# Third batch's values and late queries loaded ahead of the key and query turns, and its values cast ahead of its queries

## The chip, the cores and the metric

The kernel runs on one core of a Trainium2 chip. The metric is the time on the device in microseconds (us), the median over several executions. A separate profiled execution gives the trace from which everything about engines and transfers is read.

## The reference

Grouped-query attention followed by a gated MLP with a spatial mixing step. There are 8 batches, 16 query heads, 4 key/value heads, a sequence of 384 and a head dimension of 64. The width of the model and of the hidden layer is 1024.

```python
k = np.repeat(k, group, axis=1); v = np.repeat(v, group, axis=1)
scores = scale * np.matmul(q, k.transpose(0, 1, 3, 2))
scores = scores - np.max(scores, axis=-1, keepdims=True)
attn = np.exp(scores)
attn = attn / (np.sum(attn, axis=-1, keepdims=True) + 1e-09)
x = np.matmul(attn, v)            # then heads beside each other: [B, S, 1024]

h = np.maximum(x @ w_in, 0.0)
u, v = h[..., :512], h[..., 512:]
v_n = (v - mean(v)) / np.sqrt(var(v) + 1e-06)
v_s = np.einsum('ts,bsd->btd', w_spatial, v_n) + b_spatial[None, :, None]
out = (u * v_s) @ w_out
```

## The kernel before

One program does both parts, batch after batch, and lays the MLP of one batch beside the attention of the next. The order of instructions on every engine is written out by the program when it is built; nothing is reordered afterwards.

**Attention.** A batch is cut into 18 units: three query tiles (`qt`), two groups of heads (`j`), three key tiles (`kt`). Units are numbered through all batches, so batch 0 has 0 to 17, batch 1 has 18 to 35 and batch 2, the third, begins at 36. From unit 21 on, three units are done at a time, which I call a step and name by its first unit (24, 27, ..., 36, 39, 42). `units` issues the score matmuls (`sc`, L281) from the turned keys `kT` and the turned queries `qT`. `exp` on ScalarE gives `aT`. `weigh` (L301) multiplies with the values `v1` into `av`, and VectorE divides into `x` (L315, L317).

**MLP.** `v_part` (`pv`, L357) and `u_part` (`pu`, L438) multiply the turned `x`, named `xt`, by `w_in`. `s_part` (`psp`, L457) does the spatial mixing, and POOL multiplies into `gT` (L474). `o_part` (`po`, L496) multiplies by `w_out`. `gated` strings these together, and `pour` deals them out between the attention's instructions by a budget of TensorE time.

**How a batch's inputs get ready.** Loads bring float32 into staging tiles. They are `load_k`, `load_v` and `load_q`, and a query load can be cut by tiles: `(0,)` is the first query tile and `(1, 2)` are the late ones. POOL casts to float16 (`cast_k`, `cast_q`, `cast_v` at L187 to L208). Then the keys and queries are turned. For batches 0 and 1 TensorE turns them. From the third batch on, SP issues transposing DMAs: `k_send` (L250) and `q_send` (L258). The turned x goes the same way from batch 1 on (`x_send`, L341). The values need no turn; `cast_v` writes straight into `v1`, of which there are two, used by even and odd batches.

**What sets the order around the change.** `at(n, f, ...)` puts a call into a list under a unit number. In a step the lists of its three units are called one after the other, at one fixed place in the step, each list in the order in which it was written:

```python
for u in range(n, n + NT):
    for f, args in todo.pop(u, []):
        f(*args)
```

SP takes its DMAs one after the other, and POOL its casts and its own DMAs. So a call's place in these lists is its place in the queue of its engine. The output projection's weights `w_out` are loaded by two DMAs that POOL issues in step 24 (L169).

The third batch needs, in order: `kT` and the first tile of `qT` for `j` = 0 at step 36, the first tile of `qT` for `j` = 1 at step 39, its values in `v1` for the first `weigh` at the end of step 36, and the late tiles of `qT` for `j` = 0 at step 42.

Of the kernel before, what the change touches and what calls it, by code (L numbers as in the profile page):

```python
# [18 lines left out]
def kernel(  # L19
# [52 lines left out]
    pool, dve, act, sp = nc.gpsimd, nc.vector, nc.scalar, nc.sync  # L72
# [521 lines left out]
    def at(n, f, *args):  # L594
        todo.setdefault(n, []).append((f, args))
# [82 lines left out]

    at(20, cast_k, 2, pool)
    at(22, cast_q, 2, 0, pool, (0,))  # L680
    at(24, k_send, 2)
    at(24, q_send, 2, 0, 0, 1)
    at(26, cast_q, 2, 1, pool, (0,))
    at(26, q_send, 2, 1, 0, 1)
    at(26, load_w_out, 0, DH)
    at(26, load_w_out, DH, DM)
    at(29, load_q, 2, 0, sp, (1, 2))
    at(29, load_v, 2)
    at(31, load_q, 2, 1, sp, (1, 2))
    at(36, cast_v, 2, pool)  # L690
    for j, n in ((0, 34), (1, 36)):
        at(n, cast_q, 2, j, pool, (1, 2))
        at(n + 1, q_send, 2, j, 1, NT)
# [346 lines left out]
```

## Time and profile before

| | before |
|---|---|
| median of 3 runs | 238.40 us |
| lowest and highest | 238.39, 239.18 us |
| profiled execution, its own time | 238.65 us |
| span of the trace | 237.1 us |
| TensorE busy | 230.4 us (97%) |
| ScalarE, VectorE, POOL busy | 170.0, 143.8, 102.2 us |
| SP's DMA queue (q1), share of the 16 DMA engines' time | 68.9% |
| POOL's DMA queue (q0), the same | 12.3% |

The profiled execution takes 1.55 us longer than its span, which is what lies around the program. In the trace, PE is TensorE's matmuls and PEld its weight loads; DVE is VectorE, ACT ScalarE, POOL GpSimd and SP SyncE; SPq marks the issue of a DMA by SP, which then runs on the 16 DMA engines. L and a number is a line of the kernel.

### The profile page before, as it was taken

Reading aid. Unit: us, or ns where it says so; the run is one execution under the profiler, and the core shown is the slowest. Engines: PE = TensorE matmul, PEld = TensorE weight load, DVE = VectorE, ACT = ScalarE, POOL = GpSimd, SP = SyncE. Lnnn points to the kernel's source line nnn. Section 1 sums busy time; section 2 is a strip of 40 time slices with the busy share of each in tenths; the row PEclk is TensorE's granted clock in tenths of the full one; section 3 lists DMA queues with packets and bytes.
Section 4 is the critical chain, followed back from the end, with each engine's and each line's share of the span. In section 5 each row is a group of like instructions: output and inputs, shape, how many; then the busy total and the mean of one; then the engine's idle time right before and its main releaser. Section 6 shows DMA issues by size and latency. Waiting matters only on the chain.

```text
span 237.1 us, 5954 instructions
## 1 busy us (share of the span) xinstructions
PE 230.4 (97%) x2317; PEld 124.3 (52%) x2317; DVE 143.8 (61%) x382; ACT 170.0 (72%) x350; POOL 102.2 (43%) x149
## 2 busy tenths in 40 slices
PE   7899999999999999999999999999999999999993
PEld 6555655545554545555464555554465455545542
DVE  2668774676447674566646576376744667367561
ACT  2899989959897869977797776986697776401212
POOL 3489493642556442275045800575032500460740
PEclk9999999999999999999999999999999999999999
DMA  6999959999999999699988899479912543240266
GB/s 186 289 300 308 275 152 160 169 317 260 296 211 237 258 351 171 214 199 309 188 257 214 241 214 294 68 271 158 255 27 44 114 164 79 48 177 0 86 229 222
DMA packets 67757, 47.48 MB, mean 200 GB/s; under 512 B 48368, under 2 KB 60576, under 8 KB 67728
## 3 DMA queue, kind: packets, MB, share of 16 engines
q1 hardware_dynamic: 62800, 39.86, 68.9%
q0 software_dynamic: 3952, 6.42, 12.3%
q10 hardware_dynamic: 976, 0.82, 1.1%
q8 instruction: 18, 0.29, 0.5%
q14 instruction: 11, 0.09, 0.1%
HBM read 25.95 MB, written 12.58 MB: 163 GB/s over the span
## 4 chain that ended last, share of the span: by engine, by line
PE 91%; DMA 4%; DVE 2%; issue 0%; ACTq 0%; ACT 0%
PE pu L438 18%; PE pv L357 17%; PE po L496 17%; PE sc L281 15%; PE av L301 14%; PE psp L457 7%; DMA q<-in_q_dram 2%; DMA qT<-q 2%; PE qps L240 1%; PE xps L334 1%; DVE x L317 1%; DVE qT L218 0%; DVE osb L218 0%; DVE q L208 0%; ACTq L124 0%
## 5 line engine op out<-in xcount | busy, mean ns | idle before, releaser
L293 ACT ACTIVATE aT<-sc 128x512 f16<-128x512 f32 x288 | 147.5, 617 | 31.4 <-PE sc L281 30.8
L301 PEld LDWEIGHTS <-aT 128*128 128x128 f16 x1152 | 47.0, 97 | 17.3 <-issue 2.3
L357 PE MATMUL pv<-w_in,xt 128*128 128x512 f16 x192 | 51.0, 380 | 0.1
L301 PE MATMUL av<-v,aT 128*128 128x65 f16 x1152 | 50.5, 193 | 0.1
L496 PE MATMUL po<-w_out,gT 128*128 128x512 f16 (+2 forms) x200 | 50.5, 371 | 0.0
L438 PE MATMUL pu<-xt,w_in 128*128 128x384 f16 x256 | 49.9, 327 | 0.0
L401 POOL TENSOR_SCALAR vn<-vr,rstd,nmr 128x512 f16<-128x512 f32 x23 | 17.6, 779 | 67.0 <-DVE nmr L396 45.6
L474 POOL TENSOR_TENSOR gT<-vs,uT 128x384 f16<-128x384 f32 x31 | 32.4, 1058 | 31.8 <-DVE r_all L315 16.9
L317 DVE TENSOR_TENSOR x<-av,r_all 128x256 f16<-128x256 f32 x96 | 40.7, 424 | 3.3
L281 PE MATMUL sc<-qT,kT 64*128 64x512 f16 x288 | 41.5, 380 | 0.3
L315 DVE RECIPROCAL r_all<-av 128x4 f32<-128x4 f32 x96 | 17.1, 178 | 40.6 <-PE av L301 40.3
L218 DVE COPY osb<-po 128x512 f32<-128x512 f32 (+2 forms) x39 | 26.1, 669 | 16.3 <-PE po L496 16.3
L438 PEld LDWEIGHTS <-w_in 128*128 128x128 f16 x256 | 22.1, 98 | 17.1 <-issue 5.5
L449 ACT ACTIVATE uT<-pu 128x384 f16<-128x384 f32 x32 | 15.8, 495 | 16.0 <-PE pu L438 15.8
L496 PEld LDWEIGHTS <-gT 128*128 128x128 f16 x200 | 17.6, 98 | 17.1 <-issue 3.3
L357 PEld LDWEIGHTS <-xt 128*128 128x128 f16 x192 | 15.8, 97 | 17.8 <-issue 5.5
L281 PEld LDWEIGHTS <-kT 64*128 64x128 f16 x288 | 10.9, 94 | 23.5 <-issue 11.9
L457 PE MATMUL psp<-wsT,vn 128*128 128x384 f16 x96 | 22.2, 327 | 0.0
L469 DVE TENSOR_TENSOR vs<-psp,bias_bc 128x384 f32<-128x384 f32 x32 | 17.6, 552 | 7.1 <-PE psp L457 6.9
L371 DVE TENSOR_SCALAR vr<-pv 128x512 f32<-128x512 f32 x24 | 16.4, 682 | 8.4 <-PE pv L357 8.3
L203 POOL CAST q<-q 128x768 f16<-128x768 f32 x22 | 17.6, 830 | 7.9 <-issue 4.3
L383 DVE BATCH_NORM_STATS2 stats<-vr 128x6 f32<-128x512 f32 x24 | 16.4, 685 | 0.1
(55 smaller groups left out, 103.2 us busy)
## 6 DMA issues: line engine op xcount, KB each, us to landing
out_dram<-osb SPq DMA_DIRECT2D x20, 512.0 KB, 3.9
q<-in_q_dram SPq DMA_DIRECT2D x10, 768.0 KB, 5.7
v_None<-in_v_dram SPq DMA_DIRECT2D x6, 384.0 KB, 7.0
w_in<-in_moe_w_in_dram POOLq DMA_DIRECT2D x4, 512.0 KB, 9.8
k_None<-in_k_dram SPq DMA_DIRECT2D x5, 384.0 KB, 3.8
out_dram<-osb SPq DMA_DIRECT2D x7, 256.0 KB, 2.5
q<-in_q_dram POOLq DMA_DIRECT2D x2, 768.0 KB, 7.6
w_out<-in_moe_w_out_dram POOLq DMA_DIRECT2D x2, 512.0 KB, 9.5
```

The lines of the kernel that those rows point to most:

```text
L203: eng.tensor_copy(t16[:, :, :, hh, :], src[:, hh])
L218: (act.copy if eng is act else dve.tensor_copy)(o, i)
L281: nc.tensor.matmul(sc, kTs[b][rows, j, kt * P : (kt + 1) * P], qTs[b, j][rows, qt].rearrange("p (r i c) -> p i r c", r=G, i=G), start=True ...
L293: act.activation(a, sc, AF.Exp, scale=scale)
L301: nc.tensor.matmul(av[:, i * (D + 1) : (i + 1) * (D + 1)], aT[:, kt, hh, i * P : (i + 1) * P], v1[b % 2][:, 2 * j + hh, kt, 0 : D + 1], st ...
L317: dve.tensor_tensor(x16s[b][:, qt, c : c + 256].rearrange("p (i d) -> p i d", i=G), o[:, :, 0:D], r.to_broadcast([P, G, D]), ALU.mult,)
L357: nc.tensor.matmul(pv, xts[b][:, kt, st * P : (st + 1) * P], w_in16[:, kt, DH:DFF], start=(kt == 0), stop=(kt == NK - 1),)
L401: (dve if b == 0 and st == 1 else pool).tensor_scalar(vn, v_r.pop((b, st)), rstd[:, st : st + 1], nmr[:, st : st + 1], op0=ALU.mult, op1=A ...
L438: nc.tensor.matmul(pu[:, 0:S], w_in16[:, kt, m * P : (m + 1) * P], xts[b][:, kt, :], start=(kt == 0), stop=(kt == NK - 1),)
L457: nc.tensor.matmul(psp[:, 0:S], v_n[b, st][:, m * P : (m + 1) * P], wsT16[:, st, :], start=(st == 0), stop=(st == NT - 1),)
L474: pool.tensor_tensor(gT, vs, uT, ALU.mult)
L496: nc.tensor.matmul(po[:, 0:width], gTs[b][:, m, tt * P : (tt + 1) * P], w_out16[:, m, c0 : c0 + width], start=(m == 0), stop=(m == NM - 1),)
```

## The change

Only the lists around the third batch (batch index 2) are changed. The load of its values and the load of the late queries of its first half (`j` = 0) move from step 27 to step 24, where they are written ahead of the turn of its keys and of its first queries. The load of the late queries of its second half (`j` = 1) moves from step 30 to step 27. The cast of its values moves from step 36 to step 33, where it stands ahead of the cast of the late queries of the first half.

```diff
     at(20, cast_k, 2, pool)
     at(22, cast_q, 2, 0, pool, (0,))
+    at(24, load_v, 2)
+    at(24, load_q, 2, 0, sp, (1, 2))
     at(24, k_send, 2)
     at(24, q_send, 2, 0, 0, 1)
     at(26, cast_q, 2, 1, pool, (0,))
     at(26, q_send, 2, 1, 0, 1)
     at(26, load_w_out, 0, DH)
     at(26, load_w_out, DH, DM)
-    at(29, load_q, 2, 0, sp, (1, 2))
-    at(29, load_v, 2)
-    at(31, load_q, 2, 1, sp, (1, 2))
-    at(36, cast_v, 2, pool)
+    at(29, load_q, 2, 1, sp, (1, 2))
+    at(34, cast_v, 2, pool)
     for j, n in ((0, 34), (1, 36)):
         at(n, cast_q, 2, j, pool, (1, 2))
         at(n + 1, q_send, 2, j, 1, NT)
```

The order of SP's DMAs in this stretch becomes:

| before | after |
|---|---|
| x turn (tile 0 of batch 1) | x turn (tile 0 of batch 1) |
| keys' turn | load of values |
| first queries' turn, j = 0 | load of late queries, j = 0 |
| first queries' turn, j = 1 | keys' turn |
| load of late queries, j = 0 | first queries' turn, j = 0 |
| load of values | first queries' turn, j = 1 |
| x turn (tile 1) | load of late queries, j = 1 |
| load of late queries, j = 1 | x turn (tile 1) |
| late queries' turn, j = 0 | late queries' turn, j = 0 |

The instructions of TensorE, VectorE and ScalarE keep their order. On POOL the cast of the values and the two casts of the late queries of the first half change places.

## Prediction

> **What bounds the kernel now.** I read the page first, then the chain of waits, then the timelines of SP, POOL and TensorE from 30 to 60 us, and last the DMA packets in short stretches. The page's first part:
>
> ```profile
> PE 230.4 (97%) x2317; PEld 124.3 (52%) x2317; DVE 143.8 (61%) x382; ACT 170.0 (72%) x350; POOL 102.2 (43%) x149
> ```
>
> TensorE (PE) is busy for 230.4 of 237.1 us, so a change that leaves its instructions alone can give back only gaps, and costs whatever new gaps it makes. A busy PE can hide a stall, because a matmul's modelled end stretches over one; I therefore look at distances between starts. The chain of waits shows one non-PE piece in the middle of the run, a DMA that turns the third batch's queries:
>
> ```profile
> 50.06 0.04 issue
> 50.10 4.94 DMA qT<-q
> 55.04 0.04 issue
> 55.08 1.13 PE sc L281 x6
> 56.21 0.04 issue
> 56.25 0.81 PE pv L357 x3
> ```
>
> Columns are start, length, work. The score matmuls (`sc`) of step 42 start as that transfer lands. PE's timeline around it:
>
> ```profile
> 49.88 1.03 PE L496 MATMUL po<-w_out,gT 128*128 128x512 f16 x4
> 51.02 0.52 PE L301 MATMUL av<-v,aT 128*128 128x65 f16 x12
> ...
> 54.33 0.63 PE L301 MATMUL av<-v,aT 128*128 128x65 f16 x12
> 55.08 1.11 PE L281 MATMUL sc<-qT,kT 64*128 64x512 f16 x6
> 56.25 0.81 PE L357 MATMUL pv<-w_in,xt 128*128 128x512 f16 x3
> ```
>
> Elsewhere four `po` take 0.86 us from start to next start, twelve `av` 0.36, six `sc` 0.755 (chain of waits, 44 to 54 us). Here they take 51.02-49.88 = 1.14, 55.08-54.33 = 0.75 and 56.25-55.08 = 1.17. So three waits cost 0.28 + 0.39 + 0.41 = 1.08 us: `av` waits for the cast of the values (POOL, 50.14 to 50.97), `sc` for the late queries (landed 55.04), `pv` for the turned x of the second batch's last tile (issued 51.43, 4.4 us to landing). Added up like this, the whole stretch from 47.15 to 58.70 holds 11.55 us of which 10.27 is matmul time: 1.28 us is all there is to win in it.
>
> SP's own timeline shows what is moved, and past what:
>
> ```profile
> 33.99 1.24 SPq L341 DMA_TRANSPOSE xt<-x  x1
> 35.33 1.58 SPq L250 DMA_TRANSPOSE kT<-k  x1
> 37.00 5.39 SPq L258 DMA_TRANSPOSE qT<-q  x2
> 42.44 0.58 SPq L124 DMA_DIRECT2D q<-in_q_dram  x1
> 43.09 0.48 SPq L114 DMA_DIRECT2D v_None<-in_v_dram  x1
> 43.67 3.33 SPq L341 DMA_TRANSPOSE xt<-x  x1
> 47.04 0.58 SPq L124 DMA_DIRECT2D q<-in_q_dram  x1
> 50.10 1.23 SPq L258 DMA_TRANSPOSE qT<-q  x1
> 51.43 1.34 SPq L341 DMA_TRANSPOSE xt<-x  x1
> ```
>
> **What is moved on POOL.** The cast of the values (0.83 us) goes in front of the two late-query casts (0.61 us each). POOL ends its `gT` products at 47.45 and today waits 1.46 us for the late queries until 48.91. With both loads landed by then, the value cast runs 47.45 to 48.28 and the query casts to 49.45. The value wait (0.28) goes. The late-query turn can be issued at 49.5 instead of 50.10, 0.6 earlier, which is more than the 0.39 it costs. The last wait goes only in part: the x that is turned is ready at 50.95 (DVE), so its issue moves from 51.43 to at best 51.0, and `pv` from 56.25 to 55.82. The gain is at most 0.43 us, unless later gaps close as well.
>
> **What is moved on SP.** Two loads, 384 KB of values and 512 KB of late queries, go in front of three turns: the keys (`kT`), and the first query tiles of either half (`qT`). The load of the second half's late queries also goes in front of the x turn of 43.67. PE needs `kT` and the first `qT` for `sc` at 48.10, and could have started that at 47.79 + 0.22 = 48.01. The DMA view gives 11.2 us to landing for `kT` (35.33, so 46.5) and 10.0 for the first `qT` (37.00, so 47.0):
>
> ```profile
> kT<-k SPq DMA_TRANSPOSE x1, 11.2
> qT<-q SPq DMA_TRANSPOSE x1, 10.0
> ```
>
> The margin is 48.01 - 47.0 = 1.0 us. Issuing costs SP 0.48 + 0.58 us, which is covered, since SP stands 3.71 us in the first query turn anyway. What decides is how much later that `qT` lands. Three rows bound it. These are DMA packets, first from 37.0 to 40.5 us, then from 9 to 12 us:
>
> ```profile
> q0 software_dynamic: 534, 0.54, 111.6%
> q1 hardware_dynamic: 45, 0.00, 1.8%
> ...
> q0 software_dynamic: 356, 0.35, 72.3%
> q1 hardware_dynamic: 482, 0.47, 44.9%
> ```
>
> q1 is SP's queue, q0 POOL's. While `w_out` (q0) streams, SP's queue carries almost nothing for 3.5 us; plain loads beside weights carried 482 packets in 3 us early in the run.
> - Low end: the loads fit wholly into that emptiness and the turns are no later. Shift 0.
> - Beside `w_out`: by the code the loads are 512 + 256 = 768 packets; at 482/3 = 161 per us they take 4.8 us, 37.2 to 42.0. Meanwhile q0 gets 356/3 = 119 instead of 534/3.5 = 153 packets per us, so `w_out` falls behind by 4.8 x 34 = 163 packets, 1.1 us. Today the query turns start in bulk just where the last packets of `w_out` end (about 45.5), so they shift by 1.1.
> - By bytes: after 47.0 the same kind of load alone moved 0.36 MB in 1.0 us; 0.92 MB is 2.5 us. Shift 2.5.
> - High end: the two 256 KB loads of 8.1 us, beside `w_in`, landed by 15.5 (7.0 us after issue). Scaled to 896 KB that is 12.3 us, 47.7 from an issue at 35.4. Behind loads alone the first query turn landed 3.1 us after the last load (66.9, then 70.05, third-to-fourth batch). 50.8: shift 3.8.
>
> I take 1.8, between the two middle rows. The first `qT` then lands at 48.8 and PE stalls 0.8 us at step 36, whole on its path.
>
> The Trainium skill ("DMA: Bandwidth & Descriptors", section "Queues, rings and completion order") says that each engine consumes a queue's descriptors in ring order, which speaks against the change: turns cannot pass the loads. Taken alone it gives the 2.5 us by bytes, a stall of 1.5 and a sum of +0.7. The trace agrees on the order (the loads issued at 42.44 show their large packets only from 47.0, behind the turns) but shows an empty queue in front of them, so I do not charge the whole 2.5.
>
> The x turn of 43.67 lands at 50.87 today and is read at 51.38. It now has 512 KB more ahead (1.5 us by the same rate): 52.4 against a need of 51.38 - 0.28 + 0.8 = 51.9. Between 0 and 0.5 us late; I take 0.3. `w_out`'s halves landed 42.0 and 46.1 and are read at 47.79 and 49.88: covered even 1.8 later. The two weight-free engines, DVE and ACT, get the same instructions in the same order.
>
> **Sum.** Without waits `pv` of step 42 would start at 56.25 - 1.08 = 55.17. With the stall and the x turn, 55.17 + 0.8 + 0.3 = 56.27; the last x turn allows 55.82. So 56.27 against 56.25: nothing. The profiled execution took 238.65 (span 237.1 plus 1.55), 0.25 above the median of the three runs, 238.40. I forecast on the median: 238.4.
>
> **Rivals.**
> 1. The loads hide in the empty queue and the turns are not late. For it: 45 packets in 3.5 us. Against: `w_out` itself must slow by 1.1 us. Sum -0.43: 238.0.
> 2. The turns of keys and queries become the wait that ends last, in place of the late queries. Shift 3.8, stall 50.8 - 48.0 = 2.8, less 1.08: +1.7, 240.1. For it: the margin is 1.0 us and 0.92 MB is put in front of it while the DMA engines are already over 100% busy. Against: the rows of 9 to 12 us, where both queues together moved more than one alone. It costs anything from a landing at 49.1 (48.0 + 1.08) on, and over 0.5% (1.2 us) from 50.3 on.
> 3. The stretch closes up altogether, because the last x turn lands sooner behind a queue that is empty by then: -1.28, 237.1. Against: that turn's data are ready only at 50.95.
> 4. The change does not do what it says, the loads being held by a buffer still in use. Against: v's buffer was last read long before, and SP shows no such wait today. 238.4.
>
> **How the numbers follow.** About 0.5%, or 1.2 us, is what a measurement of this kernel tells from no change (its three runs span 0.8 us). Forecast 0.40, rival 1 0.18, rival 2 0.30, rival 3 0.08, rival 4 0.04. Slower by over 0.5% holds rival 2; faster holds rival 3; the rest is the same: 0.62. The range takes rivals 1 and 2 and some more of a stall at the top, leaves out rival 3 and a tenth at the top: 237.6 to 240.6. The likeliest case's own range is 238.0 to 239.1.
>
> **What would show it.** In the changed profile: SP issues the value load right after the x turn of 34 us; the value cast stands before the query casts and ends by 48.5; the 4.94 us piece is gone from the chain of waits, with a `kT` or `qT` landing in its place at step 36; `sc` of that step starts near 48.8. A start at 48.1 means rival 1; past 50.3, rival 2. The forecast is wrong if the end moves while step 42 does not, for then the time came from elsewhere.

## Result and profile after

The changed kernel took 239.22 us (median of 22 runs, 238.06 to 240.47), the kernel before 238.44 us (22 runs beside them, 237.77 to 239.42). The ratio is 1.0028, 95% interval 1.0015 to 1.0042: slower by 0.67 us by that ratio (the two medians lie 0.78 us apart), where no change was forecast. Two later sets of 12 runs gave 1.0035 (1.0010 to 1.0059) and 1.0035 (1.0013 to 1.0056).

The first part of the page after, to be set beside the one of before:

```profile
PE 230.6 (97%) x2317; PEld 124.4 (52%) x2317; DVE 143.6 (60%) x382; ACT 170.0 (72%) x350; POOL 102.0 (43%) x149
```

TensorE does the same work; the span of this execution is 237.7 us against 237.1. SP's timeline shows that the change does what it says (start, length in us, the DMA issued):

```profile
35.23 0.68 SPq L114 DMA_DIRECT2D v_None<-in_v_dram  x1
35.97 0.51 SPq L124 DMA_DIRECT2D q<-in_q_dram  x1
36.60 4.93 SPq L250 DMA_TRANSPOSE kT<-k  x1
41.62 4.27 SPq L258 DMA_TRANSPOSE qT<-q  x2
45.94 0.75 SPq L124 DMA_DIRECT2D q<-in_q_dram  x1
46.78 1.24 SPq L341 DMA_TRANSPOSE xt<-x  x1
```

The loads stand right behind the x turn of 34 us. The key turn, issued at 36.60, lands 11.1 us later (47.7); the first query turn, issued at 41.62, lands at 48.2, where it was 47.0 before. TensorE's timeline at the same places as in the prediction:

```profile
47.75 0.38 PE L496 MATMUL po<-w_out,gT 128*128 128x512 f16 x1
48.25 0.82 PE L281 MATMUL sc<-qT,kT 64*128 64x512 f16 x6
...
50.03 1.03 PE L496 MATMUL po<-w_out,gT 128*128 128x512 f16 x4
50.89 0.53 PE L301 MATMUL av<-v,aT 128*128 128x65 f16 x12
51.82 1.25 PE L357 MATMUL pv<-w_in,xt 128*128 128x512 f16 x5 [0.40 <-DMA xt<-x]
...
54.56 0.38 PE L357 MATMUL pv<-w_in,xt 128*128 128x512 f16 x1
...
55.35 1.30 PE L281 MATMUL sc<-qT,kT 64*128 64x512 f16 x6
56.70 0.81 PE L357 MATMUL pv<-w_in,xt 128*128 128x512 f16 x3
```

Read by distances between starts. From the single `po` to `sc` of step 36 it is 0.50 us, before 0.31: a wait of 0.19. From four `po` to `av` it is 0.86, the bare matmul time: the wait for the values' cast is gone. From `av` to the first `pv` of tile 1 it is 0.93 in place of 0.36: a new wait of 0.57 for the x turn (46.78, 5.0 us to landing). And from the last `pv` of tile 1 to `pv` of step 42 it is 56.70 - 54.56 = 2.14 us. Before it was 56.25 - 54.11 = 2.14. That is the surprise: the late queries, turned from 49.19 on, landed at 52.6 here and no longer at 55.04, and nothing of it was gained. The chain of waits says why (start, length, work):

```profile
55.41 0.61 DVE vr L371
56.02 0.04 issue
56.06 0.60 PE sc L281 x3
56.66 0.04 issue
56.70 0.81 PE pv L357 x3
```

Half of the six score matmuls wait until VectorE has evicted `pv` of tile 1 (`vr`). PSUM is the memory that matmuls write their sums to. The program deals out eight banks of it, and by its order a matmul writes a bank only when what the bank held has been read out, which is called evicting here. By the program's assignment the second `sc` of step 42 uses the bank that ScalarE's fourth exponential of step 39 empties, the third that of an `av` that VectorE evicts just before, and the fourth that of the `pv` of tile 1. The `pv` of step 42 uses the bank of the `av` that starts at 54.78, and VectorE evicts that one only behind `vr`, until 56.55:

```profile
56.13 0.42 DVE L317 TENSOR_TENSOR x<-av,r_all 128x256 f16<-128x256 f32 x1
```

So two waits for VectorE lie one behind the other there, and an earlier landing shortens neither.

**A ledger.** What follows rests on one measure that is free of the start-up: from the first `sc` of step 24 to `pv` of step 42. Without any wait for a transfer or cast it is 24.9 us (the 2.14 included). Outside of it nothing moves with the change: over all fourteen profiles here step 24 began at 30.1 to 32.4 us, in code that is the same in all, and from step 48 to the end it took 173.4 to 173.9 us.

| kernel, execution | wait at step 36 | values' cast | x turn of tile 1 | last `pv` to `pv` of 42 | sum, 24 to 42 | ratio (95% interval) |
|---|---|---|---|---|---|---|
| before, 1st | 0 | 0.28 | 0 | 2.14 | 25.18 | |
| before, 2nd | 0 | 0 | 0 | 2.13 | 24.90 | 1.0009 (0.9984 to 1.0035) |
| changed, 1st | 0.19 | 0 | 0.57 | 2.14 | 25.68 | 1.0028 (1.0015 to 1.0042) |
| changed, 2nd | 0.73 | 0 | 0.61 | 2.14 | 26.25 | 1.0035 (1.0010 to 1.0059) |
| changed, 3rd | 0.53 | 0 | 0 | 2.13 | 25.44 | 1.0035 (1.0013 to 1.0056) |
| x turn first, 1st | 0.92 | 0 | 0 | 2.14 | 25.84 | 1.0010 (0.9987 to 1.0033) |
| x turn first, 2nd | 0.57 | 0 | 0 | 2.14 | 25.49 | 1.0036 (1.0011 to 1.0061) |
| second half only | 0 | 0.04 | 1.01 | 2.14 | 25.96 | 1.0025 (0.9999 to 1.0050) |
| values only, 1st | 0 | 0 | 0 | 2.13 | 24.91 | 1.0029 (0.9999 to 1.0058) |
| values only, 2nd | 0 | 0 | 0 | 2.75 | 25.53 | 1.0017 (0.9990 to 1.0043) |
| queries only, 1st | 0 | 0 | 0 | 2.14 | 24.91 | 0.9973 (0.9953 to 0.9993) |
| queries only, 2nd | 0 | 0 | 0 | 2.20 | 24.98 | 1.0009 (0.9982 to 1.0035) |
| queries, Relu on ACT | 0 | 0 | 0 | 2.35 | 25.13 | 1.0039 (1.0012 to 1.0067) |
| turns first | 0 | 0 | 0 | 2.14 | 24.92 | 1.0005 (0.9974 to 1.0037) |

The changed kernel's mean sum is 25.79, that of before 25.04: 0.75 us, beside the measured 0.67. In these five executions the time went into this stretch and nowhere else. That the two numbers come so close is in part luck, since single executions of one kernel lie 0.3 to 0.8 us apart in it. The ratios alone say less: in the rows without a wait in the first three columns they run from 0.9973 to 1.0039, as far up as those of the changed kernel. What follows goes by the waits.

### The profile page after: what moved, and what is told of

Same layout as the page of the kernel before. It is cut to its first block, busy times and chain, and to the rows that moved or that the text cites. A ratio compares the mean times of both kernels' runs of the same rounds, so it can differ in the third digit from the quotient of the medians.

```text
span 237.7 us, 5954 instructions
## 1 busy us (share of the span) xinstructions
PE 230.6 (97%) x2317; PEld 124.4 (52%) x2317; DVE 143.6 (60%) x382; ACT 170.0 (72%) x350; POOL 102.0 (43%) x149
## 3 DMA queue, kind: packets, MB, share of 16 engines
q0 software_dynamic: 3952, 6.42, 11.9%
## 4 chain that ended last, share of the span: by engine, by line
PE 88%; DMA 8%; DVE 1%; SPq 1%; issue 0%; POOL 0%
PE pu L438 18%; PE pv L357 17%; PE po L496 17%; PE sc L281 14%; PE av L301 13%; PE psp L457 7%; DMA w_in<-in_moe_w_in_dram 4%; DMA xt<-x 2%; DMA v_None<-in_v_dram 2%; PE qps L240 1%; PE xps L334 0%; DVE x L317 0%; SPq L114 0%; DVE osb L218 0%; DVE vr L371 0%
## 5 line engine op out<-in xcount | busy, mean ns | idle before, releaser
L401 POOL TENSOR_SCALAR vn<-vr,rstd,nmr 128x512 f16<-128x512 f32 x23 | 17.7, 783 | 68.0 <-DVE nmr L396 46.5
L474 POOL TENSOR_TENSOR gT<-vs,uT 128x384 f16<-128x384 f32 x31 | 32.5, 1061 | 32.4 <-DVE r_all L315 16.8
L203 POOL CAST q<-q 128x768 f16<-128x768 f32 x22 | 17.7, 833 | 6.9 <-issue 3.7
```

What stands on the lines that cost most here:

```text
L203: eng.tensor_copy(t16[:, :, :, hh, :], src[:, hh])
L401: (dve if b == 0 and st == 1 else pool).tensor_scalar(vn, v_r.pop((b, st)), rstd[:, st : st + 1], nmr[:, st : st + 1], op0=ALU.mult, op1=A ...
L474: pool.tensor_tensor(gT, vs, uT, ALU.mult)
```

## Experiments

The first theory was that the new wait at the x turn makes the loss; the rival was that the key and first query turns do, at step 36.

**The x turn in front again.** The changed kernel with

```diff
-    at(29, load_q, 2, 1, sp, (1, 2))
+    at(31, load_q, 2, 1, sp, (1, 2))
```

> The changed kernel with one line put back: the second half's late queries (q, j = 1) are loaded in step 30 again, so behind the x turn of the second batch's tile 1. Theory (the loss comes from that x turn, put behind 512 KB more): the turn is issued near 45.9 us and lands near 50.9, the first pv of its tile starts at 51.25 instead of 51.82, pv of step 42 at about 56.1 instead of 56.70, and the time goes back by about 0.57 us, to 0.999 to 1.001 of before. Rival (the loss comes from the turns of keys and first queries landing late at step 36): nothing of that comes back, the ratio stays near 1.003, and pv of step 42 stays near 56.7.

Measured: the wait at the x turn is gone, but `sc` of step 36 started at 49.57, 0.92 us late, the largest such wait of all:

```profile
49.57 0.82 PE L281 MATMUL sc<-qT,kT 64*128 64x512 f16 x6 [0.85 <-DMA qT<-q]
```

The sum was 25.84. It did not come down as the theory had it, and the ratio of 1.001 did not tell the theories apart. In this execution POOL also issued the `w_out` loads late, at 36.57, which is 4.96 us after step 24 began (1.15 to 3.98 us in the other profiles). Both loads ahead of the turns had landed by 42.2, while the second half of `w_out` landed at 49.15 and the key turn at 49.16. This largest wait is therefore not shown to be the work of the loads alone. A second execution beside the changed kernel:

> The changed kernel with the x turn in front of the second half's late queries, once more; last time sc of step 36 waited 0.92 us and pv of tile 1 did not wait. Theory: no wait at the x turn, a wait at step 36 between 0.1 and 0.9 us, 25.0 to 25.8 us in all, ratio 1.0005 to 1.0025, below the changed kernel in the same call by about 0.6 us less what the wait at step 36 varies. Rival (the x turn is not part of the loss): the same ratio as the changed kernel.

The waits were as expected (0 and 0.57 us). The ratio was 1.0036 beside 1.0035 of the changed kernel run beside it; the 0.6 us that was to come back did not show. With the x turn in front its wait is gone and step 36 waits longer, so the mean sum is 25.67 beside 25.79 of the changed kernel. That the order of the x turn has a share of its own in the loss is not shown.

**The x turn behind, alone.** The kernel before with

```diff
-    at(31, load_q, 2, 1, sp, (1, 2))
+    at(29, load_q, 2, 1, sp, (1, 2))
```

> The kernel before with one line of the change alone: the second half's late queries are loaded in step 27, ahead of the x turn of tile 1. Nothing is put ahead of the turns of keys and first queries. Theory (x turn): it lands near 52.4 instead of 50.87 (512 KB at 0.36 MB per us are 1.5 us), pv waits for it from 51.38 to about 52.4, time +0.6 to +1.0 us, ratio 1.003 to 1.004. Rival (turns of keys and first queries): no change, ratio 1.000.

The first `pv` of tile 1 started at 52.21, just behind the x turn's landing at 52.16. So 512 KB ahead of that turn do cost when nothing else holds TensorE up: 1.01 us in this one execution. The sum rose to 25.96. The wait is real, but in the changed kernel it hides partly behind the one at step 36: the later `sc` starts there, the later the x turn is needed.

**One load ahead of the turns at a time.** The kernel before with the values' part alone:

```diff
+    at(24, load_v, 2)
     at(24, k_send, 2)
...
-    at(29, load_v, 2)
-    at(36, cast_v, 2, pool)
+    at(34, cast_v, 2, pool)
```

> The kernel before with the values' part of the change alone: their load ahead of the key turn in step 24, their cast in step 33; both loads of late queries stay where they were before. Theory (x turn, and the early values being what the change gains): av of step 36 no longer waits for the cast (0.28 us less), sc of step 36 starts by 48.3, the x turn is not late, ratio 0.998 to 1.000. Rival (turns of keys and first queries): the 384 KB delay them as much as half of the change does, sc of step 36 starts past 48.3, ratio 1.001 or more.

There was no wait at step 36. The sum fell to the floor, 24.91, while the ratio was 1.0029; step 24 began 1.4 us later than in the profile of before. Therefore once more:

> The values-only kernel (load of values ahead of the key turn, cast in step 33, late queries' loads as before) once more: its median was 1.003 of before while its profile shows no wait for a DMA on the way from step 24 to step 42 (24.91 us, before 25.18). If the profiled execution was a lucky one and the key turn behind 384 KB is late in most, a wait at step 36 of 0.3 us or more is seen now, with a ratio near 1.003. If its start-up was unlucky (step 24 began 1.4 us later than in the kernel before, in code that is the same), the ratio is 0.998 to 1.000 now.

Again no wait at step 36, and a ratio of 1.0017. But a new wait appeared, which neither theory had:

```profile
56.40 0.82 PE L357 MATMUL pv<-w_in,xt 128*128 128x512 f16 x3 [0.67 <-DMA xt<-x]
```

The issue of the late queries' turn held SP from 50.63 for 2.47 us, so the last x turn was issued only at 53.20. The two sums average 25.22, 0.18 above before, which both intervals allow.

The kernel before with the first half's late queries alone:

```diff
+    at(24, load_q, 2, 0, sp, (1, 2))
     at(24, k_send, 2)
...
-    at(29, load_q, 2, 0, sp, (1, 2))
```

> The kernel before with the first half's late queries loaded ahead of the key turn in step 24, and nothing else moved. If the late queries' landing at 55.04 really cost 0.39 us (as the prediction had it), the time falls by up to 0.39 us, ratio 0.998. If that wait only covers another one (the score matmuls of step 42 need a PSUM bank that VectorE frees when it evicts pv of tile 1), the stretch from the last pv of that tile to pv of step 42 stays at 1.9 us and the ratio is 1.000 to 1.001.

> The queries-only kernel once more (late queries of the first half loaded ahead of the key turn, nothing else moved): 24.91 us from step 24 to pv of step 42 and 0.997 of before so far. Theory: the way is 24.9 to 25.0 us again, and the ratio 0.998 to 0.9995, since the way explains only 0.27 us (0.1%) of the gain. If 0.997 holds with the same way, something before step 24 or after step 42 is faster too. Rival (512 KB ahead of the key turn are late by chance only): a wait at step 36, ratio 1.000 or more.

There was no wait at step 36 in either, and sums of 24.91 and 24.98. In the first the late queries' turn was issued at 48.66, not 50.10, but took 6.2 us and landed at 54.85, hardly before the 55.04 of before. In the second it took 6.7 us. So these runs do not take that landing away, as they were meant to, and their 2.14 settles nothing. Six other profiles do: in the three of the changed kernel, the two with the x turn first and the one with the second half only, the late queries landed 0.2 to 2.5 us before `sc` of step 42 could have started, and the distance to `pv` of step 42 was 2.13 or 2.14. The 0.39 us that the prediction gave to that landing was not there to win. The 2.20 of the second execution is a wait for the last x turn (50.78 plus 5.0 us to landing, `pv` at 55.85). The ratio was 0.9973 and then 1.0009. The first is more than the ledger can explain (0.27 us are 0.1%) and did not hold in the second, so this kernel is not shown to be faster than the one before.

**Both loads behind the turns.** The changed kernel with the two loads written after the turns of step 24, and the second half's late queries back in step 30:

```diff
-    at(24, load_v, 2)
-    at(24, load_q, 2, 0, sp, (1, 2))
...
     at(26, q_send, 2, 1, 0, 1)
+    at(26, load_v, 2)
+    at(26, load_q, 2, 0, sp, (1, 2))
...
-    at(29, load_q, 2, 1, sp, (1, 2))
+    at(31, load_q, 2, 1, sp, (1, 2))
```

> The changed kernel with the turns of keys and first queries put in front of both loads again (all still issued from step 24), and the second half's late queries loaded behind the x turn as before: what is left of the change is that the values are loaded before the late queries and cast before them. Theory (loads in front of turns are what costs at step 36): no wait at step 36, sc of that step starts 17.0 us after that of step 24; the values land near 49 us, so the wait for their cast (0.28 us) goes or shrinks; 24.9 to 25.1 us from step 24 to pv of step 42, ratio 0.998 to 1.000. Rival (step 36 is late by chance, whatever is in front): a wait at step 36 of 0.2 us or more is seen here too.

No wait at all: 24.92 us, ratio 1.0005. With the order put back the waits are gone. The time agrees, but its interval reaches up to 1.0037, so the time alone does not tell this kernel from the changed one. Together with the rows above, step 36 waits in five of five profiles that have both loads ahead of the turns (0.19 to 0.92 us) and in none of nine that have one or none.

One thing besides the loads differs between these profiles. In six of the nine, POOL issued the `w_out` loads ahead of SP's x turn of tile 0, as in the second execution of before (`w_out` at 33.20, the x turn at 33.56). In the other three, and in all five that wait, POOL issued them behind it. So like has to be set beside like. With `w_out` behind the x turn, the first query turn landed 15.7 and 15.9 us after step 24 began with no load ahead (second half only; before, 1st), 16.6 with the values ahead (values only, 2nd), and 17.2 to 17.7 with both (17.9 in the execution with the late `w_out`). With `w_out` ahead of it, it landed at 14.8 and 15.1 with no load (turns first; before, 2nd) and at 14.7 to 16.3 with one. `sc` needs it at 17.0. Two loads ahead therefore put that landing some 1.7 us later and past the need. The order of the two issues goes with another 0.8 us, and no profile here has both loads with `w_out` issued first.

**Who sets the 2.14 us.** The queries-only kernel, with one eviction on another engine:

```diff
+        if (b, st) == (1, 1):
+            act.activation(vr, pv, AF.Relu)
+        else:
             dve.tensor_scalar(vr, pv, 0.0, None, op0=ALU.max)
```

> The queries-only kernel, with one eviction moved: pv of batch 1, tile 1 is evicted by ScalarE (Relu) in place of VectorE. If the last 2.14 us from the last pv of that tile to pv of step 42 are set by VectorE's eviction, which frees the PSUM bank of the third pair of score matmuls, they fall to about 1.75, and the ratio from 0.997 to about 0.996. If they are set by the landing of the late queries or of the last x turn, they stay at 2.14.

The number was missed, the wait moved: it became 2.35 us. ScalarE takes the eviction after three exponentials and ends it at 55.30, but the fourth exponential, which empties the bank of the second `sc`, starts only behind it, and TensorE waits for that one:

```profile
54.70 0.60 ACT L372 ACTIVATE vr<-pv 128x512 f32<-128x512 f32 x1
55.20 3.04 ACT L293 ACTIVATE aT<-sc 128x512 f16<-128x512 f32 x6
55.84 0.86 PE L281 MATMUL sc<-qT,kT 64*128 64x512 f16 x5 [0.39 <-ACT aT L293]
```

So the wait is again one for a bank and not for a transfer (the late queries landed at 54.93, the last x turn at 55.75). The run does not measure what VectorE's eviction alone costs, since another bank took its place. The ratio of 1.0039 is not explained: the stretch is only 0.09 us above the mean of before, the rest to the end 0.1. Why those twelve runs were slow stays open.

**The changed kernel and the kernel before, again.**

> The changed kernel once more, for a second look at where it waits, on the chip of the runs beside it. From the runs so far the way from the first sc of step 24 to pv of step 42 is 24.91 us without any wait for a DMA, and each wait at step 36 (keys or first queries), at the cast of the values and at the first pv of tile 1 (x turn) is added to it. Theory: one or both of the waits at step 36 and at the x turn are there again, 25.3 to 26.0 us in all, and the ratio is 1.002 to 1.004. Rival (the loss comes from elsewhere, before step 24 or after step 42): that way is 24.9 to 25.2 us, and the time is up all the same.

> The kernel before against itself. Its profile so far shows one wait on the way from the first sc of step 24 to pv of step 42 (the cast of the values, 0.28 us; 25.18 us in all). Theory: again no wait at step 36 nor at the x turn, 24.9 to 25.3 us, ratio 1.000. If its own waits vary by as much as those of the changed kernel (24.9 to 26.3 us), then single profiles of the two cannot be set against each other.

> The changed kernel a third time, beside the three others. Theory: a wait of 0.4 to 0.7 us at the x turn again and one of 0.1 to 0.9 us at step 36, 25.5 to 26.4 us from step 24 to pv of step 42, ratio 1.002 to 1.004. Rival: no wait at the x turn.

The changed kernel waited at step 36 in all three executions, at the x turn in two. In the third `sc` of step 36 started at 48.59, as the first query turn landed, and the x turn (46.31 plus 5.1 us) landed at 51.40, just ahead of its reader at 51.60, which step 36 had pushed back. The kernel before lost its one wait in its second execution: the cast of the values ended at 50.22 and `av` started at 50.31 without waiting. So even the one gain that the change really makes is worth 0 to 0.28 us.

## Why the prediction was wrong

**The step that failed is the gain.** The prediction booked 1.08 us as recoverable: 0.28 for the values' cast, 0.39 for the landing of the late queries, 0.41 for the last x turn. The last two, 0.80 us together, were not to be had, because waits for PSUM banks lay behind both. Between the same two instructions lay 2.14 us in eight profiles and 2.13 in three others, with the late queries landing from 2.5 us before `sc` of step 42 could have started to 0.4 us after. The sign was in the trace of before:

```profile
54.87 0.68 DVE L371 TENSOR_SCALAR vr<-pv 128x512 f32<-128x512 f32 x1
55.61 0.10 PEld L281 LDWEIGHTS <-kT 64*128 64x128 f16 x2 [0.36 <-issue]
55.68 0.42 DVE L317 TENSOR_TENSOR x<-av,r_all 128x256 f16<-128x256 f32 x1
56.22 0.34 PEld L357 LDWEIGHTS <-xt 128*128 128x128 f16 x3 [0.51 <-DMA xt<-x]
```

VectorE's eviction ran to 55.55, and the third pair of weight loads for `sc` started at 55.61, behind the fourth `sc`. Its next eviction ran to 56.10, and the weights for `pv` were loaded from 56.22. That last line names the x turn as what ended the wait, but that turn had landed at 55.88 (51.43 plus 4.45), 0.37 us before `pv` at 56.25, so the 0.41 was not its. The prediction looked at which transfers landed near the starts and did not ask what the later `sc` and the `pv` itself waited for. The cast's 0.28 was right in one execution of before and 0 in the other, 0.14 on average.

**The costs were about right.** The shift of the first query turn was put at 1.8 us. Measured from the first `sc` of step 24 to its landing, the three changed profiles give 17.2, 17.7 and 17.5, the two of before 15.9 and 15.1: 2.0 on average, and 1.7 beside profiles with the same order of `w_out` and x turn. The stall at step 36 was put at 0.8 and was 0.19 to 0.73, mean 0.48, because the margin was larger than the 1.0 read from one execution (1.1 and 2.0). The x turn was put at 0.3 and cost 0.57, 0.61 and 0, mean 0.39. With the gain set to what it was, the prediction's own costs give 0.8 + 0.3 - 0.14 = +0.96 us, on the side that was measured.

**The empty queue was not room.** The prediction charged less than the 2.5 us by bytes because SP's queue carried almost nothing beside `w_out`. The changed profile shows the same emptiness from 37 to 39.5 us, with the load of the values issued since 35.23:

```profile
q1 hardware_dynamic: 21, 0.00, 1.2%
```

That is SP's queue: 21 packets, while the queue of `w_out` moved 364. The load had been issued and did not move. The x turn issued ahead of it landed at 40.49; what held that turn is not shown. In the third execution that turn landed at 38.92, and there 316 packets of SP's queue moved from 37 to 40.5 us, beside 358 of `w_out`. So the 1.8 us came near the measured shift in part by luck, since this reason for it did not hold.

**The rivals.** Rival 2 had the right mechanism: the key and first query turns become the wait. It was priced at +1.7, from a shift of 3.8; the shift was half of that. Rival 1 (turns not late) holds only with one load ahead, values or late queries: landings 14.7 to 16.6 us after step 24, no wait in five profiles. It needs more than one load to use up the margin, which the prediction did not try as a case. Rivals 3 and 4 did not occur.

**What was foretold and seen.** The value cast ended at 48.05, ahead of the query casts; the 4.94 us piece left the chain of waits; SP issued as drawn. On the Trainium skill's rule ("DMA: Bandwidth & Descriptors", section "Queues, rings and completion order"), that a queue's descriptors are consumed in ring order on each engine: the trace agrees, the turns landed 2.0 us later, nearer to the 2.5 us by that rule than to a free ride in the empty queue.

**What stays open.** Single profiles of one kernel differ here by up to 0.8 us in this stretch (changed: 25.44 to 26.25), so the shares of the two waits in the loss, 0.48 and 0.39, are means of three. How the `w_out` stream and the loads share the DMA engines was not separated by a run, nor how often `w_out` is issued ahead of the x turn in executions that were not profiled. The single ratios of the part kernels (0.9973 to 1.0039) do not follow their waits.

## What to carry to other kernels

A wait that ends when a transfer lands is only worth its length if nothing else would end just then: take the matmuls behind it one by one, name the PSUM bank that each needs and when that is emptied, and book the gain up to that. Small transposing transfers behind large loads in one queue were late here by 1.7 to 2.0 us for 0.92 MB, less the margin that they had; one load fitted into the margin where two did not. A queue that moves nothing need not be free: look first whether something issued earlier in it has yet to land. Where the effect is below 1%, compare the distance between two fixed instructions over several executions, not one span with another.

## What the runs showed of the hardware

- The margin of a transfer differs from one execution to the next by as much as the effect in question: the kernel before had its first query turn 1.1 and 2.0 us ahead of need in two executions of the same program.
- The start-up varied by 2.3 us (step 24 began at 30.12 to 32.44 us) in code that was the same in all fourteen profiles, while the last 174 us agreed within 0.5. What makes it differ was not looked into.
- A transposing transfer of the keys took 9.0 to 11.9 us from issue to landing beside the weights' stream, and 3.6 to 7.3 us in the later batches of the kernel before, which have no such stream.
